# Weights decoded by way of PSUM, and 20 heads with 4-byte scores, in a block-causal attention and gated MLP kernel

## The chip, the cores and the metric

The kernel runs on one core of one Trainium2 chip. A core has five engines, each with an instruction queue of its own that it works through in order: TensorE (PE, matmuls; their weight loads are PEld), VectorE (DVE), ScalarE (ACT), GpSimd (POOL) and SyncE (SP, which here only issues DMAs). SBUF is the on-chip memory of 128 partitions; PSUM is the small memory of 8 banks into which PE writes. The metric is the device time of one launch in microseconds (us), lower is better.

## The reference

Attention over 8 batches of 8 heads, 576 positions and 64 elements a head, with a mask by blocks of 64; then a two-layer MLP over all 4608 tokens with a gate.

```python
def _attn_ref(q, k, v):
    scores = np.matmul(q, k.transpose(0, 1, 3, 2)) / np.sqrt(D)
    mask = (np.arange(S)[:, None] // 64) >= (np.arange(S)[None, :] // 64)
    scores = np.where(mask, scores, -1e9)
    scores = scores - np.max(scores, axis=-1, keepdims=True)
    attn = np.exp(scores)
    attn = attn / (np.sum(attn, axis=-1, keepdims=True) + 1e-09)
    return np.matmul(attn, v)

def _moe_ref(x, w_in, w_out):          # 512 -> 2048 -> 512
    h = x @ w_in
    sp = np.maximum(h, 0.0) + np.log1p(np.exp(-np.abs(h)))
    g = h * erf(sp)
    return g @ w_out
```

The input arrays are 4-byte floats; the weights reach the kernel as 8-byte integers, two 4-byte words an element, and their values are made on the chip.

## The kernel before, in words

There are 64 heads, taken in order, and 18 token tiles of 256 tokens. A head's queries come in four tiles of 128 and a rest of 64, which two heads share (the fifth tile).

*Scores of a head.* PE multiplies (L601 for a head on the 4-byte path, which takes q and k as loaded; L603 and L604 for one on the 2-byte path, where q and k were split into a high and a low 2-byte part). DVE takes the maximum (L607), ACT the exponential (L615), POOL divides by the sum (L686) and splits the result into two 2-byte parts (L690, L691), and a transposing DMA turns them (L692, and L715 for the fifth tile). PE then multiplies by v (L756), ACT and DVE write the result x in two 2-byte parts (L761, L762). The first WIDE = 16 heads are on the 4-byte path. A head on the 2-byte path has a maximum over its q and k (L542), a scale for each group of four heads, a split on ACT and DVE (L577, L578) and six small DMAs.

*Weights.* There are 32 pieces of 128 by 512, 16 of each matrix (s = 0 and 1). `decode` loads a piece's words (L333, tile raw), lets ACT apply a rectifier with two slopes to the upper words into the piece's place in wsb (L334), lets DVE shift the lower words right by 29 bits (L336, tile sign), and lets DVE shift the place left by 3 bits and join both (L337). `measure_weights` takes a scale from all pieces of a matrix (L353). `split_weight` then makes the 2-byte high part on ACT (L344) and the low part on DVE, as value times scale minus high part (L345). The parts of piece i lie in the place before the value of piece i, so the high part of the next piece can be written only after the low part of this one has been made: the 32 splits are one chain.

*MLP.* For each token tile there are four units of 512 hidden elements. PE makes h (L438, 48 matmuls a unit, tiles m_h), ACT and DVE the gate (L398 tanh, L407 squares, L411, L418) and its two 2-byte parts (L419, L420), PE multiplies by the second matrix (L453, 24 matmuls a unit), and after the fourth unit ACT scales the result for the store (L808). L418 and L420 have one operand in PSUM.

*The order.* All instructions are entered as tasks with a duration, what they read and write, and a priority, which is a place in slots of one head. `Plan.order` simulates the engines and gives each engine its order. DEC0, DECR and SPLIT set the slots of decoding and splitting, MOE and STEP those of the token tiles, PV and FLIP those of the multiplication by v and of the division, WIDE the heads on the 4-byte path; LAND, SHARE and ASIDE are numbers of the simulated engines. PSUM banks come from one pool of eight; tokens limit how many a kind of work holds. Until the MLP has enough work, PE gets 470 warming matmuls (L832) that nothing reads.

Of the kernel before, what the change touches and what calls it, by code (L numbers as in the profile page):

```python
# [227 lines left out]
def tile_attention_moe(ctx: ExitStack, tc: tile.TileContext, qk, v, w, maskrows, mask32, out):  # L230
    nc = tc.nc
# [90 lines left out]
    def decode(s, f):  # L322

        i = place(s, f)
        raw = buf("m", [P, UW], F32, ("r0", "r1")[f % 2], f"raw{s}_{f}", NR)
# [8 lines left out]
        add("ACT", 670, lambda: nc.scalar.activation(val(), f32(top()), AF.Prelu, scale=2.0**-112, alpha=2.0**32), r=[raw], w=[k])  # L334
# [1 line left out]
        add("DVE", 420, lambda: nc.vector.tensor_scalar(out=sign(), in0=low(), scalar1=29, scalar2=None, op0=ALU.logical_shift_right), r=[raw], w=[ks])  # L336
        add("DVE", 700, lambda: nc.vector.scalar_tensor_tensor(out=bits(), in0=bits(), scalar=3, in1=sign(), op0=ALU.logical_shift_left, op1=ALU.bitwise_or), r=[ks], w=[k])  # L337

    def split_weight(s, f):

        i = place(s, f)
# [2 lines left out]
        add("ACT", 670, lambda: nc.scalar.activation(wf16(s, f, 0), home(i + 1), AF.Copy, scale=sc), r=[kv, ("wrow", s)], w=[kw])  # L344
        add("DVE", 700, lambda: nc.vector.scalar_tensor_tensor(out=wf16(s, f, 1), in0=home(i + 1), scalar=sc, in1=wf16(s, f, 0), op0=ALU.mult, op1=ALU.subtract),  # L345
            r=[kv, kw], w=[("Wl", i), ("Wx", i)])

# [325 lines left out]
    def flip(n):  # L673
# [10 lines left out]
        for i in ks:  # L684
            w_, o = (i + 1) * P, i * (i + 1) // 2 * P
            add("POOL", 20 + 2.24 * w_, lambda i=i, w_=w_, o=o: nc.gpsimd.tensor_tensor(out=p()[:, o : o + w_], in0=p()[:, o : o + w_], in1=nb()[:, 13 + i : 14 + i].broadcast_to([P, w_]), op=ALU.mult),  # L686
                r=[(nb, 12)], w=[(p, i)])
# [241 lines left out]
```

## Time and profile before

| | us |
|---|---|
| median of 3 runs | 1106.86 (1106.24 to 1108.78) |
| the profiled execution | 1116.3 |
| its span, first to last instruction | 1114.2 |
| PE busy in it | 1057.0 |
| ACT busy | 860.9 |
| DVE busy | 776.9 |
| POOL busy | 633.4 |

The profile is of one execution. A row of a group names line, engine, operation, tiles (out<-in) and shape, then busy us and the mean ns of one, then the idle time of the engine ahead of it with what ended it. A row of a line by itself gives count, minimum/median/maximum in ns, and first and last start. A row of windows gives start:end, the length, each engine's busy us with its count of instructions, PE's granted clock, the busy share of the 16 DMA engines and GB/s. A row of the chain or of the timeline begins with its start in us and its length. Matmuls are pipelined and their ends are modelled, so a busy PE isn't PE at its peak.

### The profile page before, as it was taken

Reading aid. Unit: us, or ns where it says so; the run is one execution under the profiler, and the core shown is the slowest. Engines: PE = TensorE matmul, PEld = TensorE weight load, DVE = VectorE, ACT = ScalarE, POOL = GpSimd, SP = SyncE. Lnnn points to the kernel's source line nnn. Section 1 sums busy time; section 2 is a strip of 40 time slices with the busy share of each in tenths; the row PEclk is TensorE's granted clock in tenths of the full one; section 3 lists DMA queues with packets and bytes.
Section 4 is the critical chain, followed back from the end, with each engine's and each line's share of the span. In section 5 each row is a group of like instructions: output and inputs, shape, how many; then the busy total and the mean of one; then the engine's idle time right before and its main releaser. Section 6 shows DMA issues by size and latency. Waiting matters only on the chain.

```text
span 1114.2 us, 22781 instructions
## 1 busy us (share of the span) xinstructions
PE 1057.0 (95%) x8648; PEld 705.8 (63%) x8648; DVE 776.9 (70%) x1601; ACT 860.9 (77%) x1529; POOL 633.4 (57%) x688
## 2 busy tenths in 40 slices
PE   9587788899999999999999999999999999999998
PEld 4356465666676766666675666666666667676674
DVE  6979997967777786778776867777767755334332
ACT  4455666878888888888977988878889888777774
POOL 2658888877758566657665666575747656000000
PEclk9868698999999999999999999999999999999999
DMA  9988854657765756576656756574566553200000
GB/s 294 266 191 213 189 117 95 137 124 175 152 158 91 199 130 155 114 166 148 162 143 136 185 125 164 122 177 99 126 137 140 108 119 71 69 19 20 19 20 19
DMA packets 277981, 147.59 MB, mean 132 GB/s; under 512 B 216920, under 2 KB 258904, under 8 KB 277872
## 3 DMA queue, kind: packets, MB, share of 16 engines
q1 hardware_dynamic: 270192, 139.06, 53.9%
q10 hardware_dynamic: 7680, 7.08, 2.6%
q8 instruction: 68, 1.11, 0.4%
q14 instruction: 41, 0.34, 0.1%
HBM read 54.61 MB, written 17.83 MB: 65 GB/s over the span
## 4 chain that ended last, share of the span: by engine, by line
PE 71%; DVE 17%; ACT 6%; issue 3%; ACTq 1%; SPq 1%; POOL 1%; DMA 1%; DVEq 0%; POOLq 0%
PE o L453 29%; PE m_h L438 27%; PE u L756 6%; DVE nb L607 2%; DVE wsb L337 2%; ACT m_r L407 2%; PE s L603 2%; DVE sign L336 2%; DVE wsb L345 2%; PE s L601 2%; PE s L604 2%; PE warm L832 2%; ACT p L615 1%; ACTq L581 1%; DVE nb L611 1%
## 5 line engine op out<-in xcount | busy, mean ns | idle before, releaser
L438 PE MATMUL m_h<-xh,wsb 128*128 128x256 f16 x2304 | 396.3, 273 | 2.7 <-DVE wsb L345 1.9
L438 PEld LDWEIGHTS <-wsb 128*128 128x128 f16 x3456 | 336.6, 98 | 64.0 <-issue 4.4
L407 ACT ACTIVATE m_r<-m_r,c 128x1024 f32<-128x1024 f32 x288 | 330.5, 1148 | 45.9 <-DVE m_r L411 30.0
L686 POOL TENSOR_TENSOR p<-p,nb 128x128 f32<-128x128 f32 (+3 forms) x256 | 208.7, 847 | 247.2 <-DVE nb L683 199.8
L453 PE MATMUL o<-wsb,m_gh 128*128 128x512 f16 x1152 | 336.6, 383 | 5.6 <-ACT m_gh L419 3.0
L438 PE MATMUL m_h<-xl,wsb 128*128 128x256 f16 x1152 | 314.0, 273 | 1.2 <-DVE xl L762 1.2
L453 PE MATMUL o<-wsb,m_gl 128*128 128x512 f16 x576 | 207.7, 381 | 0.0
L691 POOL TENSOR_TENSOR pz<-p,pz 128x768 f16<-128x768 f32 (+1 forms) x128 | 190.3, 1487 | 10.2
L453 PEld LDWEIGHTS <-m_gh 128*128 128x128 f16 x1152 | 111.1, 98 | 123.9 <-issue 8.5
L411 DVE SCALAR_TENSOR_TENSOR m_r<-m_r,m_r 128x1024 f32<-128x1024 f32 x72 | 95.9, 1332 | 124.6 <-ACT m_r L407 124.3
L607 DVE TENSOR_REDUCE nb<-s 128x1 f32<-128x128 f32 (+3 forms) x256 | 116.3, 481 | 69.4 <-PE s L604 45.9
L398 ACT ACTIVATE m_r<-m_h,c,bsc 128x512 f32<-128x512 f32 (+3 forms) x192 | 120.5, 677 | 25.5 <-PE m_h L438 12.3
L615 ACT ACTIVATE p<-s,nb,qsc 128x128 f32<-128x128 f32 x192 | 116.6, 612 | 24.1 <-DVE nb L611 18.1
L418 DVE SCALAR_TENSOR_TENSOR m_h<-m_r,m_h 128x512 f32<-128x512 f32 x144 | 93.1, 689 | 44.9 <-ACT m_r L407 44.5
L690 POOL CAST pz<-p 128x768 f16<-128x768 f32 (+1 forms) x128 | 115.7, 904 | 0.0
L419 ACT CAST m_gh<-m_h 128x512 f16<-128x512 f32 x144 | 81.3, 587 | 28.2 <-DVE m_h L418 22.8
L420 DVE TENSOR_TENSOR m_gl<-m_h,m_gh 128x512 f16<-128x512 f32 x144 | 93.6, 682 | 12.6 <-ACT m_gh L419 11.2
L453 PEld LDWEIGHTS <-m_gl 128*128 128x128 f16 x576 | 56.3, 98 | 59.9 <-issue 1.0
L756 PE MATMUL u<-pT,vh 128*64 128x64 f16 (+2 forms) x1408 | 84.0, 239 | 5.7 <-DMA pT<-pz 2.5
L832 PE MATMUL warm<-ident 128*128 128x256 f16 (+1 forms) x470 | 76.8, 316 | 1.5 <-POOL ident masks.py:199 1.5
L756 PEld LDWEIGHTS <-vh 128*64 128x64 f16 x1408 | 64.0, 117 | 22.0 <-issue 17.5
L756 PE MATMUL u<-pT,vl 128*64 128x64 f16 (+2 forms) x704 | 69.9, 238 | 0.0
(103 smaller groups left out, 1254.2 us busy)
## 6 DMA issues: line engine op xcount, KB each, us to landing
raw<-w SPq DMA_DIRECT2D x32, 512.0 KB, 5.9
st<-qk SPq DMA_DIRECT2D x48, 288.0 KB, 3.2
v<-v SPq DMA_DIRECT2D x16, 640.0 KB, 4.5
out<-ob SPq DMA_DIRECT2D x36, 256.0 KB, 2.6
x_d<-x SPq DMA_DIRECT2D x28, 288.0 KB, 2.8
qk<-qhi ACTq DMA_DIRECT2D x96, 72.0 KB, 2.5
qk<-qhi SPq DMA_DIRECT2D x96, 72.0 KB, 2.1
qk<-qlo SPq DMA_DIRECT2D x96, 72.0 KB, 2.2
```

Source lines behind the costliest of these rows:

```text
L398: add("ACT", 310 + 0.84 * w * (y - x) / T, lambda i=i, h=h, b=b, x=x, y=y, w=w: nc.scalar.activation(cut(br[0]()[:, i * w : (i + 1) * w], ...
L407: add("ACT", 300 + 0.834 * UW, lambda r=r, a=a, pp=pp: nc.scalar.activation(r(), a(), AF.Square, bias=const(pp[1]), scale=pp[0]), r=[a] + ...
L411: add("DVE", 160 + 1.05 * UW, lambda r=r, a=a, c=c, pp=pp, ops=ops: nc.vector.scalar_tensor_tensor(out=r(), in0=a(), scalar=pp[0], in1=c() ...
L438: nc.tensor.matmul(hk(k), lhsT=wf16(0, f, lo)[:, cc * P : (cc + 1) * P], rhs=x()[:, cc, :], start=cc == 0 and i == 0, stop=cc == NCC - 1 a ...
L453: nc.tensor.matmul(o[c](), lhsT=a()[:, sl], rhs=wf16(1, f, wlo), start=u == 0 and k == 0 and not lo and wlo == 0, stop=u == NU - 1 and k = ...
L607: add("DVE", 145 + 1.07 * w_, lambda: nc.vector.tensor_reduce(out=nb()[:, i : i + 1], in_=s()[:, c : c + w_], axis=AX.X, op=ALU.max, negat ...
L615: begun[n] = add("ACT", 538 + 0.84 * w_, lambda: nc.scalar.activation(p()[:, o : o + w_], s()[:, c : c + w_], AF.Exp, bias=nb()[:, 4 + i : ...
L686: add("POOL", 20 + 2.24 * w_, lambda i=i, w_=w_, o=o: nc.gpsimd.tensor_tensor(out=p()[:, o : o + w_], in0=p()[:, o : o + w_], in1=nb()[:, ...
L690: add("POOL", 20 + 1.12 * (z - a) * P, lambda a=a, z=z: nc.gpsimd.tensor_copy(part_(0)[:, a:z], whole()[:, a:z]), r=kp, w=[(pz, 0, i)])
L691: add("POOL", 20 + 2.24 * (z - a) * P, lambda a=a, z=z: nc.gpsimd.tensor_tensor(out=part_(1)[:, a:z], in0=whole()[:, a:z], in1=part_(0)[:, ...
L756: nc.tensor.matmul(o, lhsT=vv()[:, 2 * pp + hd, j, :], rhs=r, start=j == 0 and k == 0, stop=j == todo[-1][0] and k == 2)
L832: t = add("PE", 220 if n is None else 150, lambda: nc.tensor.matmul(b_w()[:, : w * P], lhsT=ident16, rhs=ident16[:, None, :].broadcast_to( ...
```

## The change

`decode` now lets ACT write the rectified upper words into a PSUM bank (wd), lets DVE shift that bank left by 3 bits in place, and lets DVE shift the lower words right by 29, join them with the bank and write the piece's place in wsb. The tile sign is gone. `split_weight` copies the high part into a PSUM bank (we) with a matmul by a 2-byte identity (unit, made by POOL at the start), and the low part subtracts that bank instead of the high part in SBUF. At most NW = 3 banks are held by this work. WIDE goes from 16 to 20. Nine numbers of the order change. BYACT is empty, so its branches aren't taken; LOW is 1.

```diff
-DEC0, DECR, SPLIT = (0.5, 6.5), (0.1, 0.1), 8.0
-MOE, STEP = 14.0, 0.9
+DEC0, DECR, SPLIT = (4.0, 9.0), (0.05, 0.05), 5.0
+MOE, STEP = 14.0, 0.88
...
-PV, FLIP = -2.0, 1.5
+PV, FLIP = -1.2, 1.0
...
-WIDE = 16
+WIDE = 20
+NW = 3
+BYACT = frozenset(())
+LOW = 1
...
-    LAND = 3500.0
+    LAND = 2500.0
...
-    SHARE = 0.3
+    SHARE = 0.9
...
-    ASIDE = 2.5
+    ASIDE = 0.5
...
+    unit = cpool.tile([P, P], F16, name="unit")
+    nc.gpsimd.tensor_copy(unit, ident)
...
-        bs = buf("m", [P, UW], F16, ("gh", "gl")[f % 2], f"sign{s}_{f}", NG)
-        sign = lambda: bs().bitcast(I32)
-        k, ks = ("W", i + 1), bs
+        d = bank(f"wd{s}_{f}")
+        hold = token("w", NW)
+        k = ("W", i + 1)
...
-        add("ACT", 670, lambda: nc.scalar.activation(val(), f32(top()), AF.Prelu, scale=2.0**-112, alpha=2.0**32), r=[raw], w=[k])
+        add("ACT", 670, lambda: nc.scalar.activation(d()[:, :DM], f32(top()), AF.Prelu, scale=2.0**-112, alpha=2.0**32), r=[raw, hold], w=[d])
...
-        add("DVE", 420, lambda: nc.vector.tensor_scalar(out=sign(), in0=low(), scalar1=29, scalar2=None, op0=ALU.logical_shift_right), r=[raw], w=[ks])
-        add("DVE", 700, lambda: nc.vector.scalar_tensor_tensor(out=bits(), in0=bits(), scalar=3, in1=sign(), op0=ALU.logical_shift_left, op1=ALU.bitwise_or), r=[ks], w=[k])
+        high = lambda: d()[:, :DM].bitcast(I32)
+        add("DVE", 690, lambda: nc.vector.tensor_scalar(out=high(), in0=high(), scalar1=3, scalar2=None, op0=ALU.logical_shift_left), w=[d])
+        add("DVE", 690, lambda: nc.vector.scalar_tensor_tensor(out=bits(), in0=low(), scalar=29, in1=high(), op0=ALU.logical_shift_right, op1=ALU.bitwise_or), r=[raw, d, hold], w=[k])
...
-        add("DVE", 700, lambda: nc.vector.scalar_tensor_tensor(out=wf16(s, f, 1), in0=home(i + 1), scalar=sc, in1=wf16(s, f, 0), op0=ALU.mult, op1=ALU.subtract),
-            r=[kv, kw], w=[("Wl", i), ("Wx", i)])
+        if LOW:
+            e = bank(f"we{s}_{f}")
+            hold = token("w", NW)
+            add("PE", mmns(DM, True), lambda: nc.tensor.matmul(e()[:, :DM], lhsT=unit, rhs=wf16(s, f, 0), start=True, stop=True), r=[kw, hold], w=[e])
+            add("DVE", 750, lambda: nc.vector.scalar_tensor_tensor(out=wf16(s, f, 1), in0=home(i + 1), scalar=sc, in1=e()[:, :DM], op0=ALU.mult, op1=ALU.subtract), r=[kv, kw, e, hold], w=[("Wl", i), ("Wx", i)])
```

The order of the instructions changes over the whole program. Three places show it. The first is SP's queue at the last weight loads (raw is a weight piece, pT the transposed probabilities of a head, pT_2 and the like with a place in front of their number those of a fifth tile). Before:

```order
L333 DMA raw_11_1093<-w 128x1024
L766 DMA x_d<-x_1_1084 128x2x64
L333 DMA raw_12_1117<-w 128x1024
L474 DMA v_1_1_1130<-v 128x1280
L692 DMA_TRANSPOSE pT_1140<-pz_1072 128x20x128
L715 DMA_TRANSPOSE pT_2_1178<-pz_0_108 128x10x128
L333 DMA raw_13_1192<-w 128x1024
L333 DMA raw_14_1198<-w 128x1024
L333 DMA raw_15_1201<-w 128x1024
```

And with the change (line numbers are those of the changed kernel):

```order
L338 DMA raw_11_1402<-w 128x1024
L338 DMA raw_12_1407<-w 128x1024
L706 DMA_TRANSPOSE pT_1426<-pz_1389 128x20x128
L543 DMA st_1521<-qk 128x576
L732 DMA_TRANSPOSE pT_4_1532<-pz_0_110 128x10x128
L783 DMA x_d<-x_3_1523 128x2x64
L338 DMA raw_13_1555<-w 128x1024
L338 DMA raw_14_1562<-w 128x1024
L338 DMA raw_15_1577<-w 128x1024
```

The transpose in the first piece is the 6th of a head and the 3rd of a fifth tile (pT_2), in the second the 9th and the 5th (pT_4): the last three weight pieces now stand behind three heads more.

The second place is DVE's queue where pieces 4 to 6 of the first matrix are decoded (sign, wd and raw with a piece's number; nb and s belong to heads, vs, vl and bsc to v and its scales). Before:

```order
L336 TENSOR_SCALAR sign_4_337<-raw_4_213 128x512
L337 SCALAR_TENSOR_TENSOR wsb<-wsb,sign_4_337 128x512
L336 TENSOR_SCALAR sign_5_353<-raw_5_236 128x512
L337 SCALAR_TENSOR_TENSOR wsb<-wsb,sign_5_353 128x512
L336 TENSOR_SCALAR sign_6_366<-raw_6_252 128x512
L337 SCALAR_TENSOR_TENSOR wsb<-wsb,sign_6_366 128x512
```

With the change:

```order
L342 TENSOR_SCALAR wd_4_352<-wd_4_352 128x512
L508 COPY vsb_1_408<-vb_1_405 128x2
L519 TENSOR_TENSOR bsc<-vsb_0_228,vsb_1_408 128x1
L520 RECIPROCAL bsc<-bsc 128x1
L522 TENSOR_SCALAR bsc<-vsb_0_228,bsc 128x1
L522 TENSOR_SCALAR bsc<-vsb_1_408,bsc 128x1
L343 SCALAR_TENSOR_TENSOR wsb<-raw_4_249,wd_4_352 128x512
L342 TENSOR_SCALAR wd_5_380<-wd_5_380 128x512
L513 SCALAR_TENSOR_TENSOR vl_1_436<-v_0_1_275,vsb_1_408,vh_1_416 128x1280
L343 SCALAR_TENSOR_TENSOR wsb<-raw_5_303,wd_5_380 128x512
```

Decoding a piece is two instructions as before, with the bank wd in the place of sign; piece 4 now comes among the maxima of head 3, where it came behind those of head 1, and the work on v stands between.

The third place is PE's queue at the eighth unit matmul (we is its bank, warm a warming matmul, s_0_6 and s_1_6 scores of a fifth tile, qb a scale of q and k); the kernel before has no such rows:

```order
L665 MATMUL s_0_6_1953<-qk_107 64x288
L665 MATMUL s_0_6_1953<-qk_108 64x288
L849 LDWEIGHTS ident
L849 MATMUL warm<-ident 128x256
L665 MATMUL s_1_6_1962<-qk_107 64x288
L665 MATMUL s_1_6_1962<-qk_108 64x288
L849 LDWEIGHTS ident
L849 MATMUL warm<-ident 128x256
L354 LDWEIGHTS unit
L354 MATMUL we_3_1973<-wsb,unit 128x512
L575 MATMUL qb_1976<-qrow_1941,room_82 64x2 x2
```

A step of the split chain now stands in PE's queue, behind scores and ahead of the scale of a group of heads.

More of the change, by code (lines that the diff above doesn't have):

```diff
@@ L344, in split_weight @@
         add("ACT", 670, lambda: nc.scalar.activation(wf16(s, f, 0), home(i + 1), AF.Copy, scale=sc), r=[kv, ("wrow", s)], w=[kw])
-        add("DVE", 700, lambda: nc.vector.scalar_tensor_tensor(out=wf16(s, f, 1), in0=home(i + 1), scalar=sc, in1=wf16(s, f, 0), op0=ALU.mult, op1=ALU.subtract),
-            r=[kv, kw], w=[("Wl", i), ("Wx", i)])
+        if LOW:
[3 more added lines that the diff above has]
+            add("DVE", 750, lambda: nc.vector.scalar_tensor_tensor(out=wf16(s, f, 1), in0=home(i + 1), scalar=sc, in1=e()[:, :DM], op0=ALU.mult, op1=ALU.subtract), r=[kv, kw, e, hold], w=[("Wl", i), ("Wx", i)])
+        else:
+            add("DVE", 750, lambda: nc.vector.scalar_tensor_tensor(out=wf16(s, f, 1), in0=home(i + 1), scalar=sc, in1=wf16(s, f, 0), op0=ALU.mult, op1=ALU.subtract), r=[kv, kw], w=[("Wl", i), ("Wx", i)])
     def measure_weights(s):
@@ L685, in flip @@
             w_, o = (i + 1) * P, i * (i + 1) // 2 * P
+            if n in BYACT:
+                add("ACT", 220 + 0.84 * w_, lambda i=i, w_=w_, o=o: nc.scalar.activation(p()[:, o : o + w_], p()[:, o : o + w_], AF.Copy, scale=nb()[:, 13 + i : 14 + i]), r=[(nb, 12)], w=[(p, i)])
+                continue
             add("POOL", 20 + 2.24 * w_, lambda i=i, w_=w_, o=o: nc.gpsimd.tensor_tensor(out=p()[:, o : o + w_], in0=p()[:, o : o + w_], in1=nb()[:, 13 + i : 14 + i].broadcast_to([P, w_]), op=ALU.mult),
@@ L704, in flip4 @@
         add("DVE", 150, lambda: nc.vector.reciprocal(out=nb()[:, 5:6], in_=nb()[:, 5:6]), w=[(nb, 5)])
-        add("POOL", 20 + 2.24 * S, lambda: nc.gpsimd.tensor_tensor(out=p(), in0=p(), in1=nb()[:, 5:6].broadcast_to([P, S]), op=ALU.mult), r=[(nb, 5)], w=[(p, 0), (p, 1)])
+        if 2 * m + 1 in BYACT:
+            add("ACT", 220 + 0.84 * S, lambda: nc.scalar.activation(p(), p(), AF.Copy, scale=nb()[:, 5:6]), r=[(nb, 5)], w=[(p, 0), (p, 1)])
+        else:
+            add("POOL", 20 + 2.24 * S, lambda: nc.gpsimd.tensor_tensor(out=p(), in0=p(), in1=nb()[:, 5:6].broadcast_to([P, S]), op=ALU.mult), r=[(nb, 5)], w=[(p, 0), (p, 1)])
         def each(a, b):
```

## The prediction

> **What bounds the kernel now.** I read the page's chain of work that ended last first, by engine, then the windows, then single rows.
>
> ```profile
> PE 71%; DVE 17%; ACT 6%; issue 3%; ACTq 1%; SPq 1%; POOL 1%; DMA 1%; DVEq 0%; POOLq 0%
> ```
>
> Over the whole span TensorE (PE) is the bound, but an average hides two stages. The windows (busy time of PE, PEld, DVE, ACT, POOL in us with the count of instructions, then the granted clock, the DMA share and GB/s) separate them:
>
> ```profile
> 0.00:56.00 56.00, 42.42 (x221) 23.77 (x221) 44.34 (x85) 26.00 (x56) 25.31 (x42) 0.92 0.98 279
> 56.00:98.00 42.00, 34.36 (x264) 23.49 (x264) 35.32 (x87) 26.11 (x69) 27.64 (x29) 0.71 0.78 187
> 98.00:140.00 42.00, 32.00 (x214) 20.64 (x213) 40.59 (x83) 23.07 (x58) 36.57 (x37) 0.74 0.95 208
> 140.00:182.00 42.00, 35.90 (x328) 24.58 (x325) 41.25 (x77) 27.79 (x60) 36.01 (x37) 0.95 0.54 109
> 182.00:224.00 42.00, 38.69 (x324) 25.18 (x323) 34.24 (x65) 31.84 (x65) 34.33 (x35) 0.91 0.60 124
> 224.00:252.00 28.00, 26.11 (x241) 18.45 (x239) 19.09 (x43) 22.26 (x41) 20.00 (x23) 1.00 0.61 130
> 252.00:588.00 336.00, 332.32 (x2881) 225.12 (x2879) 249.76 (x537) 286.06 (x515) 221.76 (x239) 1.00 0.65 149
> 588.00:952.00 364.00, 357.24 (x3082) 239.76 (x3082) 254.06 (x553) 305.42 (x537) 231.74 (x252) 0.99 0.58 130
> ...
> sum 224.00, PE 76.83 PEld 48.77; mean PE 25.61 PEld 16.26
> ```
>
> From 252 us on PE idles 10.4 of 700 us: there PE's work sets the end. Before 224 us PE idles 40.6 us, and the last row (the warming matmuls of L832 alone) says that 76.8 us of its busy time does nothing for the output. In that stage DVE sets the pace: it is busy 40.6 and 41.3 of 42 us from 98 to 182, and the chain from 26 to 218 us, by line, runs a third of the time through three of its lines:
>
> ```profile
> by line: DVE wsb L337 11.6%; DVE wsb L345 11.3%; DVE sign L336 11.0%; PE s L601 9.7%; DVE nb L607 7.4%; issue 5.6%; PE u L756 5.3%; PE warm L832 4.0%; PE o L453 3.9%; DVE vm L481 3.6%; DVE nb L611 3.5%; PE m_h L438 2.5%; DVE vl L502 2.1%; P
> ```
>
> The second limit there, until 140 us, is DMA, with shares of 0.98, 0.78 and 0.95.
>
> So the end is the time at which the first stage hands over, plus PE work left. I mark the handover by DVE's first score maximum of head 18. Both orders have this instruction between the gates of token tile 0's last unit and tile 1's first, so about the same PE work lies behind it. In the trace:
>
> ```profile
> 249.84 1.08 DVE L607 TENSOR_REDUCE nb<-s 128x1 f32<-128x128 f32 x3
> ```
>
> **The change part by part.** *Decode and split on DVE.* Each of 32 pieces of weight has three DVE instructions, before and now.
>
> ```profile
> L336 DVE TENSOR_SCALAR sign<-raw 128x512 int32<-128x512 int32 x32 | 25.8, 810 | 0.0
> L337 DVE SCALAR_TENSOR_TENSOR wsb<-wsb,sign 128x512 int32<-128x512 int32 x32 | 32.6, 1020 | 1.3
> L345 DVE SCALAR_TENSOR_TENSOR wsb<-wsb,wrow 128x512 f16<-128x512 f32 x32 | 36.4, 1137 | 2.2 <-ACT wsb L344 2.2
> ...
> L336 DVE TENSOR_SCALAR sign<-raw x32: 404/812/1867, 13.4 to 126.8; 128x512 int32<-128x512 int32 x32
> L337 DVE SCALAR_TENSOR_TENSOR wsb<-wsb,sign x32: 659/846/2121, 14.9 to 132.7; 128x512 int32<-128x512 int32 x32
> L345 DVE SCALAR_TENSOR_TENSOR wsb<-wsb,wrow x32: 739/1134/2130, 76.0 to 217.7; 128x512 f16<-128x512 f32 x32
> ...
> L418 DVE SCALAR_TENSOR_TENSOR m_h<-m_r,m_h x144: 674/689/697, 171.8 to 1102.8; 128x512 f32<-128x512 f32 x144
> L420 DVE TENSOR_TENSOR m_gl<-m_h,m_gh x144: 658/680/693, 179.3 to 1104.1; 128x512 f16<-128x512 f32 x144
> ```
>
> The three old rows read and write SBUF alone, and their longest is three to five times their shortest (minimum/median/maximum in ns). L418 and L420, of the same width but with one operand in PSUM, vary by 35 ns at most in 144 cases each, with POOL busy beside them. I conclude that the spread is time lost to POOL, and that an instruction with a PSUM operand doesn't lose it. The three new ones all have one: shift PSUM to PSUM, join SBUF and PSUM to SBUF, low part SBUF and PSUM to SBUF. None of these forms is in the trace. Bounds are 404 ns (the fastest L336) and 1020 ns (the mean L337); I take 689 ns, L418, which reads and writes PSUM and is nearest. Old: 25.8 + 32.6 + 36.4 = 94.8 us. New: 96 × 0.689 = 66.1 us. **DVE saves 28.7 us**, all ahead of head 18; with the bounds, from 56 us saved to 3 us lost.
>
> The Trainium skill, "VectorE: DVE Perf Modes", section "Why PSUM operands drop a tier", speaks against this: a PSUM operand keeps a 4-byte operation at one element per cycle, while a 4-byte shift of SBUF runs at two. The trace agrees with the fast case (404 ns for L336 against 659 for L337), and by that rule alone the sum is that of the fifth case below.
>
> *Heads 16 to 19 on the 4-byte path* drop their scaling, splitting and 24 small loads. Ahead of head 18 the new order has one L542 and one L578 less, and some scalar rows: about 2.8 us of DVE.
>
> *DVE alone* thus brings head 18 to 249.8 − 31.5, **about 219 us**.
>
> *ACT.* Prelu now writes PSUM.
>
> ```profile
> L334 ACT ACTIVATE wsb<-raw 128x512 f32<-128x512 f32 x32 | 20.9, 668 | 13.8 <-DMA raw<-w 13.7
> L398 ACT ACTIVATE m_r<-m_h,c,bsc 128x512 f32<-128x512 f32 x96 | 72.0, 781 | 16.1 <-PE m_h L438 10.2 <-DMA qk<-qhi 3.0 <-issue 1.7
> ```
>
> L398, with its PSUM operand, is 113 ns longer; either way (±3.6 us over 32) it lies in ACT's idle time, 89 of 224 us. The one POOL copy that makes the 2-byte identity stands ahead of all heads, where POOL waits; uncovered it is under 1 us.
>
> *DMA.* The order of SP's queue shows what moves: ahead of the last weight load stand 9 head transposes and 5 of the fifth tiles instead of 6 and 3, and three more loads of q and k. The decode has been put later, behind the heads.
>
> ```profile
> q1 hardware_dynamic: 34921, 32.09, 90.6%
> ...
> pT<-pz SPq DMA_TRANSPOSE x11, 4.8
> ...
> 130.19 0.65 ACT L334 ACTIVATE wsb<-raw 128x512 f32<-128x512 f32 x1
> 132.70 0.68 DVE L337 SCALAR_TENSOR_TENSOR wsb<-wsb,sign 128x512 int32<-128x512 int32 x1
> ...
> L607 DVE TENSOR_REDUCE nb<-s 128x1 f32<-128x128 f32 (+3 forms) x256 | 116.3, 481 | 69.4 <-PE s L604 45.9 <-PE s L601 16.7 <-POOL p L686 2.8
> ...
> L578 DVE SCALAR_TENSOR_TENSOR qlo<-st,qsc,qhi 128x576 f16<-128x576 f32 x48 | 51.4, 1071 | 4.8 <-ACT qhi L577 4.6
> ```
>
> The first row is of 0 to 140 us, the second of 140 to 224; the rows with a time in front are the last weight's. Until 140 us the queue is busy 90.6%, so three heads more aren't free. From 140 to 224 us, without weights, DMA worked 0.54 × 42 + 0.60 × 42 = 48 us, for 11 transposes, which are 7 heads and 4 fifth tiles: 6.8 us a head, 20 us for three. Spare before 130 us are about 9 us (the share of 0.78 in 56 to 98). The last weight, used by ACT at 130.2 us and joined at 132.7, would then be joined some 11 us later, near 143 us. From the last join to head 18 the trace has 117 us. Between the same two points the new order has 31 low parts at 0.689 for 28 at 1.137 us (−10), two heads less of maxima (8 × 0.481) and of small rows and x tiles (−9 together), and one v tile and two L578 less (−4): 93 us more than 143, so head 18 at 236 us. The 6.8 us hold loads that both orders have, so 236 is an upper end. I take the middle of 219 and 236: **228 us, 22 us earlier**.
>
> *PE.* Ahead of head 18 come 32 unit matmuls and two 4-byte heads, covered by the warming matmuls and the idle time; uncovered, 32 × 0.216 = 6.9 us. Behind it, two heads (18, 19) double their score matmuls.
>
> ```profile
> 8.64 2.16 PE s L601 x8
> 282.59 2.62 PE m_h L438 x24
> 1095.32 14.48 PE o L453 x67
> ```
>
> One 4-byte head (four matmuls with their weight loads) is 2.16 us; at 14.48 / 67 = 0.216 us for 512 columns of 2 bytes, the 2 × 1280 columns of a 2-byte head take 1.08 us. Two heads and their fifth tile: 2 × 1.08 + 0.5, about +2.7 us.
>
> **Sum:** −22 + 2.7 = −19 us. The profiled execution took 1116.3 us with a span of 1114.2; the median of the runs shown is 1106.9. I carry the difference over unchanged: 1097 for a profiled execution, **1088 us** for the runs.
>
> **The rivals.** *All of the relief arrives* (chance 0.2). DMA hides the three heads; head 18 comes at 219 us: −31 + 2.7 = −28, 1079 us. DVE idles 37 of the first 252 us; a quarter of that saved as well gives 1070. Against it: the DMA row of 90.6%.
>
> *The gain is given back later* (0.15). The whole program has a new order, because the planner's numbers changed too. PE's idle time of 10.4 us after 252 us may double, which leaves −19 + 10 = −9 us, 1098; at 19 us more nothing is left. For it: PE's queue is in order, so one load or row put too early in the plan stops all of it. Against it: PE work is put much as before.
>
> *The split chain becomes the bound* (0.11). High part on ACT, unit matmul on PE, low part on DVE, then the next high part, since it overwrites what the low part has read.
>
> ```profile
> 140.00:224.00 84.00, 32.24 (x28) 0.93 0.57 116
> 217.73 1.13 DVE L345 SCALAR_TENSOR_TENSOR wsb<-wsb,wrow 128x512 f16<-128x512 f32 x1
> ```
>
> The first row is L345 alone. 28 low parts from 140 to 218 us are 2.8 us a step now. PE's queue is in order: a unit matmul that stands behind a block of 24 m_h matmuls (2.62 us) waits for it, behind it wait the rest of PE, and DVE at the low part. In the new order head 18 follows the last low part by some 4 us. If the chain begins at 140 us, the kernel is slower from the point where head 18 comes after 249.8 − 2.7 = 247 us, which is (247 − 4 − 140) / 32 = 3.2 us a step. With half a block of wait, 1.3 us, on 2.8 it is 4.1 us a step, head 18 at 275 us, +25 + 2.7 = +28, **1135 us, slower**. Against it: the low part is 0.45 us shorter, and the order spaces the matmuls out.
>
> *The change does not do what it says* (0.04): what POOL takes from DVE is taken from other rows instead, and only the fastest durations count. Then 404 + 659 + 739 = 1802 ns become 3 × 689 = 2067: 32 × 0.265 = +8.5, with +2.7 behind it +11, 1118 us. Against it: L418 and L420 never lose time.
>
> **How the numbers follow.** The forecast has 0.5, and by itself holds 1079 to 1096 (head 18 from 219 to 236). The range that leaves no more than 2 in 10 out reaches down to most of the full relief (1070) and up to most of what is given back (1105); the two slower cases stay outside. A measurement of this kernel tells about 0.2%, 2.2 us, from no change. Faster: 0.5 + 0.2 + 0.1 of the third case = 0.80. The same: 0.05 of the third. Slower: 0.11 + 0.04 = 0.15.
>
> **What would show it.** In the profile after: shift, join and low part near 0.69 us with almost no spread (step one); the last weight joined after 133 us if DMA holds it as I think, before if not; head 18's first maximum near 228 us; PE's idle time after it near 10 us; low parts at most 3 us apart. Wrong, if the new rows spread to 1 us and more, if DVE waits long for unit matmuls, or if PE has new idle time after 252 us.

## The result and the profile after

| | before | after |
|---|---|---|
| median of 4 runs, us | 1107.82 (1106.24 to 1109.31) | 1081.51 (1080.18 to 1082.63) |
| the profiled execution, us | 1116.3 | 1081.8 |
| its span, us | 1114.2 | 1080.0 |
| first maximum of head 18, us | 249.84 | 223.68 |
| from there to the end of the span, us | 864.4 | 856.3 |

The changed kernel takes 0.9762 of the time before (95% interval 0.9743 to 0.9782), 26.3 us less. The profiled execution of before was 8.5 us longer than this median, that of after is at its median, so the profiles differ by more (34.2 us of span) than the runs do; before's time goes with the granted clock of the execution (0.966 in its profile; of the 13 runs of before beside the first experiments, the two at 0.965 took 1115.4 and 1115.6 us, the nine at 0.973 to 0.978 took 1107.0 to 1109.5). Line numbers from here on are those of the changed kernel: L339 is the rectifier, L342 the shift, L343 the join, L350 the high part, L354 the unit matmul, L355 the low part, L618 a score maximum, L849 a warming matmul.

The chain of work that ended last, by engine for the whole span, and by line for 26 to 218 us:

```profile
PE 82%; DVE 10%; ACT 4%; issue 2%; DMA 1%; ACTq 1%; POOL 0%; SPq 0%; DVEq 0%; POOLq 0%
...
by line: PE m_h L449 11.6%; PE s L612 8.0%; PE warm L849 7.4%; DVE nb L618 6.8%; PE u L773 6.5%; DVE wd L342 6.1%; issue 5.6%; DVE wsb L343 4.2%; PE o L464 3.7%; DMA pT<-pz 3.4%; PE we L354 3.0%; DVE vm L492 2.9%; ACT m_r L418 2.3%; ACT p L
```

In the first stage the three lines of DVE that carried a third of the chain now carry about a tenth (the shift 6.1 and the join 4.2%, the low part less than the row shows), and PE lines lead it. The windows, with the bounds and columns of those shown of before:

```profile
0.00:56.00 56.00, 52.25 (x324) 29.38 (x324) 44.93 (x105) 26.02 (x70) 39.91 (x63) 1.00 1.00 271
56.00:98.00 42.00, 35.42 (x339) 25.24 (x339) 36.99 (x92) 28.83 (x71) 32.21 (x37) 0.96 1.01 240
98.00:140.00 42.00, 34.93 (x284) 24.34 (x285) 37.63 (x92) 27.12 (x63) 27.73 (x32) 0.76 0.90 238
140.00:182.00 42.00, 40.95 (x363) 27.30 (x362) 36.28 (x83) 36.97 (x79) 38.91 (x44) 1.00 0.67 137
182.00:224.00 42.00, 40.58 (x295) 25.73 (x294) 28.28 (x58) 33.92 (x59) 19.76 (x24) 0.96 0.44 82
224.00:252.00 28.00, 28.00 (x233) 18.46 (x231) 18.86 (x42) 22.05 (x41) 19.49 (x21) 1.00 0.61 152
252.00:588.00 336.00, 331.93 (x2884) 225.30 (x2882) 246.27 (x535) 286.89 (x512) 217.61 (x235) 1.00 0.66 143
588.00:952.00 364.00, 363.36 (x3137) 245.69 (x3136) 239.58 (x523) 304.23 (x527) 217.50 (x236) 1.00 0.58 127
```

Three things changed. DVE, which was full from 98 to 182 us, has 4 to 14 us free in each window from 98 to 224 us. DMA has shares of 1.00 and 1.01 until 98 us (records of packets overlap, so a share may pass 1), where it had 0.98 and 0.78. PE's idle time after 252 us fell from 10.4 to 4.7 us. The rows of the new instructions (mean of one, then minimum/median/maximum), and the marks of the stage:

```profile
L355 DVE SCALAR_TENSOR_TENSOR wsb<-wsb,wrow,we 128x512 f16<-128x512 f32 x32 | 23.8, 743 | 11.3 <-PE we L354 11.2
...
L342 DVE TENSOR_SCALAR wd<-wd 128x512 int32<-128x512 int32 x32 | 22.0, 688 | 1.2 <-ACT wd L339 1.1
L343 DVE SCALAR_TENSOR_TENSOR wsb<-raw,wd 128x512 int32<-128x512 int32 x32 | 21.9, 686 | 0.9
...
L342 DVE TENSOR_SCALAR wd<-wd x32: 668/690/700, 16.0 to 128.1; 128x512 int32<-128x512 int32 x32
L343 DVE SCALAR_TENSOR_TENSOR wsb<-raw,wd x32: 675/687/694, 16.7 to 128.9; 128x512 int32<-128x512 int32 x32
L355 DVE SCALAR_TENSOR_TENSOR wsb<-wsb,wrow,we x32: 716/746/749, 126.9 to 220.6; 128x512 f16<-128x512 f32 x32
...
128.86 0.69 DVE L343 SCALAR_TENSOR_TENSOR wsb<-raw,wd 128x512 int32<-128x512 int32 x1
220.56 0.75 DVE L355 SCALAR_TENSOR_TENSOR wsb<-wsb,wrow,we 128x512 f16<-128x512 f32 x1 [0.79 <-PE we L354]
223.68 1.09 DVE L618 TENSOR_REDUCE nb<-s 128x1 f32<-128x128 f32 x3
```

The spread is gone: 33 ns at most between shortest and longest, where the old rows spread over 1.4 us. The 96 instructions take 67.7 us instead of 94.8. The last weight is joined at 128.9 us, the last low part starts at 220.6, head 18 at 223.7.

### The profile page after: what moved, and what is told of

It reads as the page before. It is cut to its first block, busy times and chain, and to the rows that moved or that the text cites. A ratio compares the mean times of both kernels' runs of the same rounds, so it can differ in the third digit from the quotient of the medians.

```text
span 1080.0 us, 22825 instructions
## 1 busy us (share of the span) xinstructions
PE 1051.2 (97%) x8675; PEld 702.3 (65%) x8675; DVE 734.5 (68%) x1584; ACT 856.4 (79%) x1525; POOL 613.1 (57%) x689
## 4 chain that ended last, share of the span: by engine, by line
PE 82%; DVE 10%; ACT 4%; issue 2%; DMA 1%; ACTq 1%; POOL 0%; SPq 0%; DVEq 0%; POOLq 0%
PE m_h L449 33%; PE o L464 32%; PE u L773 6%; PE s L612 2%; PE warm L849 2%; PE s L614 2%; DVE nb L618 2%; PE s L615 2%; DVE wd L342 1%; PE s L671 1%; ACT m_r L418 1%; DVE wsb L343 1%; DVE nb L622 1%; ACT p L626 1%; DMA pT<-pz 1%
## 5 line engine op out<-in xcount | busy, mean ns | idle before, releaser
L700 POOL TENSOR_TENSOR p<-p,nb 128x128 f32<-128x128 f32 (+3 forms) x256 | 205.9, 835 | 255.3 <-DVE nb L694 190.4
L618 DVE TENSOR_REDUCE nb<-s 128x1 f32<-128x128 f32 (+3 forms) x256 | 116.0, 482 | 79.1 <-PE s L615 59.3
L626 ACT ACTIVATE p<-s,nb,qsc 128x128 f32<-128x128 f32 (+3 forms) x176 | 106.7, 611 | 17.2 <-DVE nb L622 12.2
L704 POOL CAST pz<-p 128x768 f16<-128x768 f32 (+1 forms) x128 | 100.9, 788 | 0.0
L431 DVE TENSOR_TENSOR m_gl<-m_h,m_gh 128x512 f16<-128x512 f32 x144 | 93.2, 683 | 11.2 <-ACT m_gh L430 9.4
L430 ACT CAST m_gh<-m_h 128x512 f16<-128x512 f32 x144 | 81.0, 586 | 20.5 <-DVE m_h L429 14.4
L773 PE MATMUL u<-pT,vh 128*64 128x64 f16 (+2 forms) x1408 | 80.4, 232 | 3.2 <-DVE m_gl L431 1.8
L849 PE MATMUL warm<-ident 128*128 128x256 f16 (+1 forms) x470 | 77.1, 311 | 1.5 <-POOL ident masks.py:199 1.5
L773 PEld LDWEIGHTS <-vh 128*64 128x64 f16 x1408 | 60.9, 112 | 21.9 <-issue 18.9
L849 PEld LDWEIGHTS <-ident 128*128 128x128 f16 x470 | 47.9, 104 | 32.3 <-issue 16.9
```

The costliest lines, as they stand in the source:

```text
L618: add("DVE", 145 + 1.07 * w_, lambda: nc.vector.tensor_reduce(out=nb()[:, i : i + 1], in_=s()[:, c : c + w_], axis=AX.X, op=ALU.max, negat ...
L626: begun[n] = add("ACT", 538 + 0.84 * w_, lambda: nc.scalar.activation(p()[:, o : o + w_], s()[:, c : c + w_], AF.Exp, bias=nb()[:, 4 + i : ...
L704: add("POOL", 20 + 1.12 * (z - a) * P, lambda a=a, z=z: nc.gpsimd.tensor_copy(part_(0)[:, a:z], whole()[:, a:z]), r=kp, w=[(pz, 0, i)])
L773: nc.tensor.matmul(o, lhsT=vv()[:, 2 * pp + hd, j, :], rhs=r, start=j == 0 and k == 0, stop=j == todo[-1][0] and k == 2)
L849: t = add("PE", 220 if n is None else 150, lambda: nc.tensor.matmul(b_w()[:, : w * P], lhsT=ident16, rhs=ident16[:, None, :].broadcast_to( ...
```

## The experiments

All start from the changed kernel. Where nothing else is said, every engine's order is that of the changed kernel, instruction by instruction (with an operand moved or a matmul repeated or left out in place). Times are medians with the ratio to the kernel before on the same chip; before took 1107.8 to 1111.9 us on the chips used, so ratios are compared, or kernels that ran on one chip. "Head 18" is the start of its first maximum in the profile; it is left empty where the order is another one.

| kernel | us | ratio, 95% interval | last join | head 18 |
|---|---|---|---|---|
| after | 1081.51 | 0.9762 (0.9743 to 0.9782) | 128.9 | 223.7 |
| decode in SBUF | 1096.95 | 0.9877 (0.984 to 0.9914) | 141.5 | 238.1 |
| low part from SBUF | 1089.42 | 0.9829 (0.978 to 0.9877) | 127.9 | 230.9 |
| both in SBUF | 1104.76 | 0.9952 (0.9933 to 0.9972) | 143.3 | 246.0 |
| unit matmul three times | 1096.25 | 0.9881 (0.9846 to 0.9917) | 130.0 | 236.9 |
| both in SBUF, POOL does less | 1096.87 | 0.9865 (0.9848 to 0.9882) | 137.0 | 238.8 |
| two free matmuls ahead of each | 1095.60 | 0.9857 (0.9842 to 0.9872) | 129.9 | 235.9 |
| old numbers of the order | 1096.23 | 0.9863 (0.9846 to 0.9881) | 125.0 | |
| 16 heads on the 4-byte path | 1088.35 | 0.9784 (0.9768 to 0.9801) | 129.5 | |
| low part from SBUF, no unit matmuls | 1091.20 | 0.9830 (0.9789 to 0.9871) | 129.5 | 231.7 |
| last warming matmuls cut | 1086.84 | 0.9797 (0.9764 to 0.9831) | 128.8 | 226.5 |
| both of the last two | 1091.04 | 0.9828 (0.9796 to 0.9860) | 131.7 | 233.0 |
| after once more, on their chip | 1083.62 | 0.9765 (0.9736 to 0.9794) | 128.6 | 223.3 |

### Decode, split, and both put back into SBUF

My theory (A in the texts below): the operands in PSUM are the gain, since the instructions no longer lose time to POOL. The rival (B): the new order is the gain, and the operands don't matter. In the first kernel the rectifier writes the piece's place again, and the shift works there:

```diff
-        add("ACT", 670, lambda: nc.scalar.activation(d()[:, :DM], f32(top()), AF.Prelu, scale=2.0**-112, alpha=2.0**32), r=[raw, hold], w=[d])
+        add("ACT", 670, lambda: nc.scalar.activation(val(), f32(top()), AF.Prelu, scale=2.0**-112, alpha=2.0**32), r=[raw, hold], w=[d])
...
-        high = lambda: d()[:, :DM].bitcast(I32)
+        high = bits
```

> The changed kernel with its order kept instruction by instruction; only the decode stays in SBUF: the rectifier writes the weight's place in SBUF, the shift works there in place, the join reads the raw words and that place. The low part still goes by way of PSUM. Theory A (an instruction of VectorE whose operands all lie in SBUF loses time to GpSimd, one with a PSUM operand doesn't): shift and join spread from about 0.4 and 0.66 to 2 us, means near 0.8 and 1.0 as in the kernel before, instead of 0.69 and 0.69: about 0.45 us x 32 = 14 us more of VectorE before the last weight, head 18 some 10 to 14 us later, 1090 to 1096 us. Theory B (the gain comes from the new order and from 20 heads, not from PSUM): the shift runs at its fastest, 0.4 us, the join at 0.66; 1081 us or up to 8 us less.

Or the low part subtracts the high part in SBUF, while the unit matmul still runs:

```diff
-            add("DVE", 750, lambda: nc.vector.scalar_tensor_tensor(out=wf16(s, f, 1), in0=home(i + 1), scalar=sc, in1=e()[:, :DM], op0=ALU.mult, op1=ALU.subtract), r=[kv, kw, e, hold], w=[("Wl", i), ("Wx", i)])
+            add("DVE", 750, lambda: nc.vector.scalar_tensor_tensor(out=wf16(s, f, 1), in0=home(i + 1), scalar=sc, in1=wf16(s, f, 0), op0=ALU.mult, op1=ALU.subtract), r=[kv, kw, e, hold], w=[("Wl", i), ("Wx", i)])
```

> The changed kernel with its order kept; only the low part subtracts the high part in SBUF, as before. The unit matmul still runs, but nothing reads its bank. Theory A: low parts spread from 0.74 to 2 us, mean near 1.1 instead of 0.746: 32 x 0.37 = 12 us more of VectorE between the last weight and head 18; 1088 to 1094 us. Theory B: low parts near 0.75 us and, without the wait for the matmul, 11 us less waiting of VectorE: 1072 to 1081 us.

Or both edits together:

> Both of the above: the order, the 20 heads and the unit matmuls of the changed kernel, with decode and low part in SBUF. What is left between this and the kernel before is the order and the heads. Theory A: head 18 some 22 to 27 us later than in the changed kernel, 1101 to 1109 us, so PSUM is the whole gain. Theory B: 1070 to 1083 us.

The groups and the minimum/median/maximum of the kernel with both:

```profile
L343 DVE SCALAR_TENSOR_TENSOR wsb<-raw,wsb 128x512 int32<-128x512 int32 x32 | 36.3, 1135 | 0.9
L355 DVE SCALAR_TENSOR_TENSOR wsb<-wsb,wrow 128x512 f16<-128x512 f32 x32 | 35.0, 1093 | 3.4 <-ACT wsb L350 3.3
...
L342 DVE TENSOR_SCALAR wsb<-wsb 128x512 int32<-128x512 int32 x32 | 22.4, 701 | 0.7 <-ACT wsb L339 0.7
...
L342 DVE TENSOR_SCALAR wsb<-wsb x32: 395/551/1756, 15.6 to 142.9; 128x512 int32<-128x512 int32 x32
L343 DVE SCALAR_TENSOR_TENSOR wsb<-raw,wsb x32: 677/978/2009, 16.7 to 143.3; 128x512 int32<-128x512 int32 x32
L355 DVE SCALAR_TENSOR_TENSOR wsb<-wsb,wrow x32: 732/950/2170, 140.7 to 242.2; 128x512 f16<-128x512 f32 x32
```

All three times came as theory A had them (1096.95 us 1 us above its range), none as B. With the order unchanged, the operands alone bring the old spread back. The ratios add up: the decode in SBUF takes back 0.0115, the low part 0.0067, both 0.0190 of the 0.0238 that was won. Head 18 comes 14.4, 7.2 and 22.3 us later, for 26.0 us more on DVE with both. The rest, 0.0048 with an interval of 0.002, is what new order and 20 heads bring without PSUM operands (and with the unit matmuls still issued). So the operands are most of the gain, though not the shift: its mean is 701 ns in SBUF and 688 in PSUM. The join (1135 to 686) and the low part (1093 to 743) are the whole of it. The loss doesn't move to other DVE rows either: DVE's busy time over the whole execution is 763.3 us with both in SBUF and 734.5 in after, 28.8 less, of which these three lines are 26.0.

The Trainium skill, "SBUF — State Buffer", section "Who interferes with whom", says that a DVE instruction with two SBUF inputs contends with GpSimd instructions that read SBUF, and one with at most one SBUF input, outside the modes that use two ports, doesn't. The rows agree: the join and the low part have one tensor input in SBUF now (the low part also a column of wrow as its scalar), and vary by 19 and 33 ns.

### POOL given less to do

Is it POOL that takes the time? Beside both edits above, POOL multiplies only the first 16 columns of each query tile for heads 0 to 17, so this kernel leaves most of their probabilities undivided:

```diff
-            add("POOL", 20 + 2.24 * w_, lambda i=i, w_=w_, o=o: nc.gpsimd.tensor_tensor(out=p()[:, o : o + w_], in0=p()[:, o : o + w_], in1=nb()[:, 13 + i : 14 + i].broadcast_to([P, w_]), op=ALU.mult),
+            c_ = 16 if n < 18 else w_
+            add("POOL", 20 + 2.24 * w_, lambda i=i, c_=c_, o=o: nc.gpsimd.tensor_tensor(out=p()[:, o : o + c_], in0=p()[:, o : o + c_], in1=nb()[:, 13 + i : 14 + i].broadcast_to([P, c_]), op=ALU.mult),
```

> The run with decode and low part in SBUF once more (1104.8 us), its order kept, and for the heads 0 to 17 GpSimd multiplies only the first 16 columns of each query tile by 1/sum (the rest is left undivided, so this part of the computation is left out). It takes some 2.8 us per head from GpSimd, more than a quarter of its work while weights are decoded. Theory A (time lost to GpSimd): shift, join and low part lose less, means of about 0.7, 0.85 and 1.0 us instead of about 0.8, 1.0 and 1.15, and the rows at which GpSimd is idle are at 0.41, 0.68 and 0.74; the end 8 to 15 us earlier, 1089 to 1097 us. Theory E (the spread comes from something else, such as DMA writing to SBUF): means unchanged within 0.05 us, 1100 to 1105 us.

Its groups:

```profile
L355 DVE SCALAR_TENSOR_TENSOR wsb<-wsb,wrow 128x512 f16<-128x512 f32 x32 | 31.3, 979 | 3.9 <-ACT wsb L350 3.8
L343 DVE SCALAR_TENSOR_TENSOR wsb<-raw,wsb 128x512 int32<-128x512 int32 x32 | 29.1, 909 | 0.9
...
L342 DVE TENSOR_SCALAR wsb<-wsb 128x512 int32<-128x512 int32 x32 | 22.9, 716 | 2.4 <-ACT wsb L339 2.4
```

The windows of the kernel with both in SBUF, then of this one (POOL's busy time is the fifth):

```profile
0.00:130.00 130.00, 110.55 (x783) 69.87 (x784) 112.42 (x236) 65.49 (x165) 96.84 (x114) 0.87 0.98 240
```

```profile
0.00:130.00 130.00, 113.81 (x816) 72.32 (x817) 107.66 (x246) 68.68 (x174) 76.02 (x119) 0.88 0.96 246
```

With 21 of POOL's 97 us taken away, join and low part lose 226 and 114 ns in the mean, and 0.9% of the time comes back (in which POOL's own relief may have a part). That is theory A's range; by theory E the means would have stayed within 50 ns. The shift doesn't follow (716 ns, 15 more). So I counted each DVE row of the traces as beside POOL or alone, by whether a POOL instruction ran at the same time (mean ns, count):

| | shift beside | alone | join beside | alone | low beside | alone |
|---|---|---|---|---|---|---|
| before | 965 (23) | 414 (9) | 1253 (19) | 679 (13) | 1177 (29) | 745 (3) |
| both in SBUF | 766 (26) | 419 (6) | 1260 (25) | 690 (7) | 1174 (26) | 742 (6) |
| and POOL does less | 851 (22) | 418 (10) | 1059 (19) | 689 (13) | 1163 (18) | 741 (14) |
| after | 687 (28) | 698 (4) | 685 (26) | 688 (6) | 741 (25) | 747 (7) |

Alone, join and low part of the new order take as long in SBUF as with an operand in PSUM, to 6 ns; only the loss beside POOL goes. The shift is another case: alone it is much faster in SBUF (419 for 698 ns), beside POOL somewhat slower (766 for 687), and the mean is even.

### What bounds the stage after the last weight

DVE has 72.95 us busy of the 94 from 130 to 224 us now (windows below), so something else must set head 18. Three runs ask whether it is the split chain with its new matmul, or PE's queue as a whole. First each unit matmul three times:

```diff
-            add("PE", mmns(DM, True), lambda: nc.tensor.matmul(e()[:, :DM], lhsT=unit, rhs=wf16(s, f, 0), start=True, stop=True), r=[kw, hold], w=[e])
+            add("PE", mmns(DM, True), lambda: [nc.tensor.matmul(e()[:, :DM], lhsT=unit, rhs=wf16(s, f, 0), start=True, stop=True) for _ in range(3)], r=[kw, hold], w=[e])
```

> The changed kernel with its order kept, and each of the 32 unit matmuls issued three times into the same bank: 0.43 us more at each step of the split chain. Theory C (after the last weight the chain of high part, unit matmul and low part is the bound): head 18 comes 32 x 0.43 = 14 us later, 1090 to 1096 us. Theory D (VectorE's own work is the bound, the chain has slack): VectorE's waits for the unit matmul grow, but the end by 0 to 4 us, 1081 to 1086 us.

Then two matmuls more ahead of each, which read only unit and don't wait for the high part:

```diff
-            add("PE", mmns(DM, True), lambda: nc.tensor.matmul(e()[:, :DM], lhsT=unit, rhs=wf16(s, f, 0), start=True, stop=True), r=[kw, hold], w=[e])
+            add("PE", mmns(DM, True), lambda: [nc.tensor.matmul(e()[:, :DM], lhsT=unit, rhs=r, start=True, stop=True) for r in (unit[:, None, :].broadcast_to([P, 4, P]), unit[:, None, :].broadcast_to([P, 4, P]), wf16(s, f, 0))], r=[kw, hold], w=[e])
```

> The changed kernel with its order kept; ahead of each unit matmul two more matmuls of 512 columns go into the same bank, whose operand is constant, so that they need not wait for the high part. TensorE gets as much more work as in the run with three unit matmuls (1096.3 us), the chain of high part, unit matmul and low part only where TensorE is late. Theory C (the chain is the bound after the last weight, TensorE waits in it): 1082 to 1087 us. Theory F (TensorE's own queue is the bound there): as with three unit matmuls, 1093 to 1097 us.

The 64 added matmuls are 64 × 0.216 = 13.8 us of PE. Head 18 came 13.2 us later in the first and 12.2 in the second, so theory D (DVE's own work is the bound) is refuted. The two kernels differ less than they were meant to: in the second, too, the first matmul of a step started before the end of its high part in only 1 of 32 steps, so they lengthened the chain there as well, and the times alone don't tell C from F. What tells them apart is who waits. Idle time of PE and PEld ahead of the unit matmuls of after, by what ended it (us, times):

```profile
  ACT p L626: 1.5, 2
  issue: 1.4, 5
  PE warm L849: 0.3, 1
  ACT wsb L350: 0.2, 1
```

PE waited for a high part (L350) once, 0.2 us: it nearly always comes to the step late, from other work in its queue. Windows of after, then of the second kernel:

```profile
130.00:177.00 47.00, 45.64 (x400) 31.18 (x399) 40.16 (x108) 39.48 (x86) 40.97 (x48) 1.00 0.67 137
177.00:224.00 47.00, 45.28 (x377) 29.46 (x375) 32.78 (x64) 38.60 (x70) 24.58 (x29) 0.96 0.41 76
```

```profile
130.00:177.00 47.00, 46.29 (x409) 31.92 (x407) 35.47 (x94) 34.90 (x78) 35.16 (x42) 1.00 0.51 106
177.00:224.00 47.00, 45.43 (x332) 27.94 (x330) 32.13 (x66) 33.98 (x65) 29.21 (x34) 1.00 0.52 105
```

PE is busy 90.9 of 94 us in after: with DVE relieved, PE's queue has become the bound of this stage (theory F). DVE waits for it at the low part; waits of after from 129 to 224 us (total us, times, longest):

```profile
DVE wsb L355 <- PE we L354: 11.2, 12, 2.1
ACT wsb L350 <- DVE wsb L355: 8.0, 9, 1.7
```

If PE is the bound, should the unit matmuls not go again, with the low part from SBUF? That is the third run, and the place where PE's bound and DVE's meet:

```diff
-            add("PE", mmns(DM, True), lambda: nc.tensor.matmul(e()[:, :DM], lhsT=unit, rhs=wf16(s, f, 0), start=True, stop=True), r=[kw, hold], w=[e])
-            add("DVE", 750, lambda: nc.vector.scalar_tensor_tensor(out=wf16(s, f, 1), in0=home(i + 1), scalar=sc, in1=e()[:, :DM], op0=ALU.mult, op1=ALU.subtract), r=[kv, kw, e, hold], w=[("Wl", i), ("Wx", i)])
+            add("PE", mmns(DM, True), lambda: None, r=[kw, hold], w=[e])
+            add("DVE", 750, lambda: nc.vector.scalar_tensor_tensor(out=wf16(s, f, 1), in0=home(i + 1), scalar=sc, in1=wf16(s, f, 0), op0=ALU.mult, op1=ALU.subtract), r=[kv, kw, e, hold], w=[("Wl", i), ("Wx", i)])
```

> The changed kernel with its order kept; the low part subtracts the high part in SBUF (as in the run that gave 1089.4 us) and the 32 unit matmuls are not issued at all. Theory F (after the last weight TensorE's queue is the bound): 32 x 0.22 = 7 us and the waits at them go, so that the unit matmul costs about what the low part by way of PSUM saves: 1079 to 1084 us, within 3 us of the changed kernel. Theory A alone (VectorE's lost time decides there): as with the unit matmuls, 1087 to 1091 us.

The windows of this kernel, and ACT's wait for low parts from 129 to 224 us:

```profile
130.00:177.00 47.00, 41.09 (x352) 28.30 (x350) 40.91 (x93) 33.23 (x75) 38.50 (x39) 0.89 0.56 100
177.00:224.00 47.00, 40.91 (x307) 26.00 (x308) 37.16 (x68) 36.20 (x69) 37.13 (x38) 0.93 0.51 107
...
ACT wsb L350 <- DVE wsb L355: 15.6, 13, 2.8
```

It took 0.9830, as with the matmuls in (0.9829; the intervals are some 0.004 to each side), and head 18 came at 231.7 us for 230.9. So theory F missed here, and theory A had it right: with the low part back in SBUF, PE has 12 us free (at a granted clock of 0.89 and 0.93) and nothing is gained, while ACT waits 15.6 us for low parts, for 8.0 in after. The low part sets the pace again, with DVE at 78 of 94 us. On its chip this kernel is 7.6 us slower than after (1083.62). So the unit matmuls, 32 × 0.216 = 6.9 us of PE by the prediction's price, are a good price for low parts that are 9.8 us shorter in sum (1049 to 743 ns with the matmuls in; 1090 to 743 without, 11.1 us).

### Warming matmuls cut

The window of the warming matmuls alone in after (PE, PEld, then the clock):

```profile
130.00:177.00 47.00, 11.05 (x79) 7.57 (x79) 1.00 0.67 137
```

They are 11 us in a stage that PE bounds, and nothing reads them. The last 89 of the 470 are left out:

```diff
+    sent = []
+
+    def fill(w):
+        sent.append(w)
+        if len(sent) <= 381:
+            nc.tensor.matmul(b_w()[:, : w * P], lhsT=ident16, rhs=ident16[:, None, :].broadcast_to([P, w, P]), start=True, stop=True)
...
-        t = add("PE", 220 if n is None else 150, lambda: nc.tensor.matmul(b_w()[:, : w * P], lhsT=ident16, rhs=ident16[:, None, :].broadcast_to([P, w, P]), start=True, stop=True), w=[b_w])
+        t = add("PE", 220 if n is None else 150, lambda: fill(w), w=[b_w])
```

> The changed kernel with its order kept, without the last 89 of the 470 warming matmuls, those that stand behind the first unit matmul. Theory F: TensorE has up to 89 x 0.11 = 10 us less in its queue between the last weight and head 18; the end 4 to 9 us earlier, 1072 to 1078 us. If they only fill TensorE's waits: 1080 to 1082 us; slower than that if the granted clock falls without them.

Without unit matmuls and with the low part from SBUF as well:

> Both of the above: no unit matmul, low part in SBUF, no warming matmul behind the place of the first unit matmul. Theory F: TensorE is relieved of 17 us, so VectorE's lost time becomes the bound again: 1076 to 1082 us, no better than the cut of the warming matmuls alone. If both add: 1070 to 1075 us.

And after unaltered, as the control on that chip:

> The changed kernel itself, unaltered, so that the three runs beside it can be read against it on one chip: a ratio of 0.976 to the kernel before, 1080 to 1086 us.

Windows of the control, then of the kernel with only the cut:

```profile
130.00:177.00 47.00, 45.58 (x401) 30.90 (x400) 40.00 (x108) 39.59 (x85) 41.28 (x48) 1.00 0.64 135
```

```profile
130.00:177.00 47.00, 41.27 (x305) 25.12 (x304) 37.89 (x104) 36.73 (x83) 40.72 (x48) 0.83 0.67 132
```

PE was left some 11 us of matmuls less, but was busy only 4.3 us less, and head 18 came 3.2 us later; the kernel took 1086.84 us against 1083.62, with intervals that overlap. The gain of 4 to 9 us that theory F had from the cut didn't come. The granted clock fell from 1.00 to 0.83 in the mean, by stretches at half the clock. Two neighbouring stretches of this kernel, and its m_h matmuls in each:

```profile
149.60:156.30 6.70, 6.69 (x22) 4.13 (x22) 3.64 (x12) 4.19 (x10) 6.54 (x9) 0.50 0.74 106
156.40:170.00 13.60, 11.04 (x122) 7.67 (x121) 11.45 (x20) 12.84 (x27) 12.05 (x13) 1.00 0.60 98
...
L449 PE MATMUL m_h<-xh,wsb 128*128 128x256 f16 x9 | 3.2, 421 | 0.0
L449 PE MATMUL m_h<-xh,wsb 128*128 128x256 f16 x23 | 4.5, 272 | 0.0
```

At half the clock an m_h matmul took 421 ns in the mean, at the full clock 272, so the work behind the cut took longer; that this alone used up the gain is argued from these rows, and no run shows it by itself. The Trainium skill, "TensorE: Matmul & The Clock Gate", Part 1, says that the hardware sets the clock by how busy PE has been, and the two rows from 130 to 177 us agree (45.58 of 47 us busy at 1.00, 41.27 at 0.83). So the warming matmuls are no idle time to put other work in for nothing. The kernel with both cuts (0.9828) is where the one without the warming cut was (0.9830): it has 0.79 for 0.89 of the clock from 130 to 177 us and isn't slower, as the low part sets the pace there. Both its forecasts, 1076 to 1082 and 1070 to 1075 us, missed.

### The order and the 20 heads

Two kernels have an order of their own. The new operations with the old numbers and 16 heads:

```diff
-DEC0, DECR, SPLIT = (4.0, 9.0), (0.05, 0.05), 5.0
-MOE, STEP = 14.0, 0.88
+DEC0, DECR, SPLIT = (0.5, 6.5), (0.1, 0.1), 8.0
+MOE, STEP = 14.0, 0.9
...
-PV, FLIP = -1.2, 1.0
+PV, FLIP = -2.0, 1.5
...
-WIDE = 20
+WIDE = 16
...
-    LAND = 2500.0
+    LAND = 3500.0
...
-    SHARE = 0.9
+    SHARE = 0.3
...
-    ASIDE = 0.5
+    ASIDE = 2.5
```

> The operations of the changed kernel (decode and low part by way of PSUM, three banks) with all numbers of the kernel before: WIDE 16, DEC0, DECR, SPLIT, STEP, PV, FLIP, LAND, SHARE, ASIDE. The planner makes its own order. If PSUM is the whole gain, 1084 to 1090 us. If the new numbers are needed for it (the early decode holds raw buffers and banks while heads wait), 1095 to 1105 us.

And the new numbers, with 16 heads:

```diff
-WIDE = 20
+WIDE = 16
```

> The changed kernel with WIDE at 16; the planner makes its own order. Heads 16 to 19 then need 2 x 1.3 us more of VectorE and ScalarE each and 24 small loads, and 1.1 to 1.3 us less of TensorE each. If TensorE is the bound from head 11 on: 1076 to 1081 us. If VectorE is: 1084 to 1088 us.

With the old numbers the new operations take 0.9863 (1096.23 us, where the second forecast had 1095 to 1105), so they bring 0.0137 by themselves and 0.0238 with the new numbers, while the new numbers bring 0.0048 without PSUM operands. The order that suits the relieved DVE is worth more beside it than alone. The 20 heads by themselves are worth some 0.002 (0.9784 to 0.9762), with intervals that overlap, so that nothing and 0.005 are both possible; which of its two forecasts holds isn't told by 1088.35 us, on a chip where before took 1111.9. Which of the other numbers brings the 1% wasn't tried.

## Why the prediction came out as it did

The forecast was 1088 us; the runs took 1081.5, inside its range. For a profiled execution it said 1097, and that took 1081.8.

- **Decode and split on DVE: right, and shown to be most of the gain.** Taken: 0.689 us for all three, 66.1 us. Measured: 0.688, 0.686 and 0.743, 67.7 us. The low part was 54 ns too short, 1.7 us in all. The reason given (time lost to POOL, from which a PSUM operand is free) holds for join and low part. For the shift the prediction counted 0.12 us saved a piece; in the changed order it would have taken 0.701 us in SBUF, so the operand itself saved it 13 ns.
- **ACT: right.** The rectifier into PSUM takes 637 ns in the median, for 666 before, and stays hidden (DVE waited for it once, 1.1 us).
- **DMA: the mis-sized term.** The prediction charged 6.8 us of DMA for each of three heads more ahead of the last weight, 20 us, less 9 of spare, and put the last join near 143 us. It came at 128.9, before the 132.7 of the kernel before. Summed over the trace's packets, a DMA engine had worked 121.8 us when before's last weight landed at 130 us, and 130.0 us when after's landed at 127: all that stood ahead of the last weight, the three heads with their loads among it, cost 8 us more, not 20. (6.8 us a head was taken from a stage in which other transfers run as well.) The spare took all of it:

```profile
q1 hardware_dynamic: 39342, 33.97, 101.7%
```

That is the queue from 0 to 128 us; before it had 90.6% until 140 us.

- **The handover: 223.7 us, for 228 forecast.** The first 14 us of error, at the last join, were mostly made good, by luck, by taking the middle of two ends, 219 and 236. From the last join to head 18 the forecast had 93 us and the trace has 94.8, but for another reason than given: it was worked out as DVE's work, and DVE has 21 us free there. PE's queue sets it.
- **PE: the cover was named wrongly.** The unit matmuls were to be covered by warming matmuls and idle time. From the last weight on they aren't: 13.8 us of further matmuls cost 12 to 13 us, and cutting warming matmuls made no room. So the 6.9 us are most likely paid for there, by a stage that DVE had left shorter by more; no run has the low part by way of PSUM without them.
- **Behind head 18: the sign was wrong.** Forecast 2.7 us more, for the doubled score matmuls; the trace has 8.1 us less (856.3 for 864.4). PE's idle time after 252 us went from 10.4 to 4.7 us, and that is 5.7 of it. All kernels of this order have 856 to 860 us behind head 18, with or without PSUM operands, so it comes from the order, or from the profiled execution of before, which was long; which of them stays open, since before has only that one profile.
- **From profile to runs.** The prediction carried the 9.4 us between before's profiled execution and its median over unchanged; after has 0.3. That takes back 9 of the 15 us by which head 18 (4 us) and the stage behind it (11 us) were off: 1088 came nearer than its terms, by luck.

Of the rivals, the full relief (head 18 at 219 us, 1079 us) is nearer to the runs than the forecast (2.5 us off, for 6.5): its premise that DMA hides the three heads was right, but head 18 is 4.7 us later, since PE sets it. The gain wasn't given back later. The split chain didn't become the bound of the whole: it takes (220.6 − 126.9) / 31 = 3.0 us a step in the mean (single steps up to 5.4, where the prediction wanted at most 3), under the 3.2 from which it would have been slower, and it began at 127 and not at 140 us; the waits of 11.2 us for unit matmuls are what there is of that rival. That only the fastest durations count is refuted: DVE's other rows didn't grow, and even the shift, whose fastest row is 395 ns in SBUF, costs as much there in the mean (701 ns) as in PSUM (688).
